# Pooled attention and a gated feed-forward layer: K and V loads issued by GpSimd on its own DMA queue, order of work searched anew

## The chip, the cores and the metric

The kernel runs on one core of a Trainium2 chip. The metric is the device time of one execution in microseconds (us), lower is better. Engines are named as in the profile: PE is TensorE (matmuls; PEld is its weight load), DVE is VectorE, ACT is ScalarE, POOL is GpSimd and SP is SyncE, which does nothing here but issue DMAs.

## What is computed

Inputs are `q`, `k`, `v` of shape (8, 8, 576, 64) and four weight matrices, all 32-bit floats (the weights arrive as 64-bit floats and are narrowed on the chip). Cut to what matters:

```
k_p = k.reshape(B, H, 72, 8, 64).mean(axis=3)          # 8 neighbouring keys are averaged
v_p = v.reshape(B, H, 72, 8, 64).mean(axis=3)
scores = q @ k_p.T / 8                                  # 576 x 72 for each batch and head
attn   = softmax(scores) @ v_p
x = attn as (4608 tokens, 512)
h = (x @ w1) * (x @ w2) @ w3                            # 512 -> 1024 -> 1024
out = h @ w_out                                         # 1024 -> 512
```

## The kernel before

**Tiling.** The 4608 tokens are cut into 12 chunks of 384. `w3` and `w_out` are multiplied into one matrix at the start, so each chunk needs `a = w1.T x`, `b = w2.T x`, their product, and one more product with the combined matrix. Each is done as three matmuls on a high and a low part of every number (`PASSES`), which is why almost every result is followed by a copy on ACT (the high part: `g_hi`, `te_post`, `mix_hi`) and a subtraction on DVE (the low part: `g_lo` at L815, and so on). Chunks 0 to 7 run plainly (L785, L833). Chunks 8 to 11 are taken two at a time and use seven block products instead of eight (`prod`, L962); their mixed weights are made during the first stage by POOL (`mix`, L882 to L884), split by ACT (`mix_hi`, L888) and DVE, and written to DRAM (L897).

**A product unit of chunks 8 to 11.** The seven products of a unit go through three accumulators in PSUM, the tags `a`, `b` and `c`. Tag `a` has one buffer: `s1_copy` (L968) and `s2_copy` (L976) on ACT, and `c22` (L987) and `g_second` (L995) on DVE, must have read it before the next product goes in. `c12` (L983) and `g_first` (L990) stand ahead of `c22` on DVE.

**Attention of a batch.** K of a batch comes in four loads (`load_k`, L390, 288 KB each), V in two (`load_v`, L457, 512 KB each) and four small ones (`load_vr`, L463, 32 KB each). All land in `st`, a pool with four buffers. Summing over the eight neighbours is done by DVE in one reduction (`pool_red`, L468) for the loads named in `K_RED` and `V_RED`, otherwise by POOL in three additions (`pool_tree`, L471 to L473). Transposed scores of the later chunks go out to DRAM and come back transposed (`te_out` L667, `te_in` L689), then `te_post` (L703, L705) splits them.

**What sets the order.** Nothing is left to a scheduler: each step is put on a list by `at(kind, k, fn, ...)` with a due time `k`, the list is sorted once, and every engine executes its own instructions in that order, each waiting at its turn for what it needs. The table `SHIFT` moves single steps by parts of a unit of `k`. Other tables choose the engine: `SOFT_ACT` (softmax of a tile mostly on ACT, or with a subtraction and sums on DVE), `MIX_DVE`, `K_RED`, `V_RED`. In the kernel before, all loads and all stores but one are issued by SP.

Of the kernel before, what the change touches and what calls it, by code (L numbers as in the profile page):

```python
# [19 lines left out]
def kernel(  # L20
# [14 lines left out]
    nc = tc.nc  # L35
# [3 lines left out]
    P = 128  # L39
# [3 lines left out]
    KR = KP - KM  # L43
# [17 lines left out]
    SOFT_ACT = [(0, 0), (0, 1), (1, 0), (1, 1), (1, 2), (1, 3), (2, 1), (2, 2), (3, 1), (3, 2), (4, 1), (4, 2),  # L61
        (4, 3), (5, 0), (5, 1), (5, 2), (6, 0), (6, 1), (6, 2), (7, 1), (7, 3), (8, 1), (8, 2), (9, 1), (9, 2),
        (10, 1), (10, 2), (10, 3), (11, 1), (11, 2)]
    HALF = [(0, 2), (2, 0), (3, 0), (4, 0), (5, 0), (6, 0), (7, 0), (8, 0), (9, 0), (10, 0), (10, 2), (11, 0)]
# [7 lines left out]
    GLO_POOL = []  # L72
    MIX_DVE = []
    MIXLO_POOL = []
    TELO_POOL = []
    K_RED = [(2, 2), (2, 3), (3, 1), (3, 2), (3, 3), (4, 0), (4, 1), (4, 2), (4, 3), (5, 1), (5, 2), (5, 3), (6,
        1), (6, 3), (7, 1), (7, 2), (7, 3)]
    V_RED = [(5, 0), (5, 1)]
    XLO_POOL = []
# [30 lines left out]
        out=msk,  # L110
        in_=ident.rearrange("p (q j e) -> p j q e", j=4, e=KR),
# [36 lines left out]
    def st_tile(shape):  # L148
        return stp.tile(shape, F32, tag="st", name="st")
# [237 lines left out]
    def load_k(b, i):  # L387
        t = stage["k", b, i] = st_tile([P, 2, POOL, D])
        if b >= 2:
            nc.sync.dma_start(  # L390
                out=t[:KP], in_=k_in[b, 2 * i:2 * i + 2].rearrange("a (k e) d -> k a (e d)", e=POOL))
        elif i < 2:
            nc.sync.dma_start(out=t.rearrange("k a e d -> k a (e d)"), in_=pair_rows(k_in, b)[KR:KR + P, 2 * i:2 * i + 2])
        else:
            for par in range(2):
                nc.sync.dma_start(
                    out=t[32 * par:32 * par + 32, 0].rearrange("k e d -> k (e d)"),
                    in_=rest_rows(k_in, b, 0, (KR + P) * par, [(2 * KP, NPR), (1, KR)]))
# [56 lines left out]
    def load_v(b, hf):  # L455
        t = stage["v", b, hf] = st_tile([P, 2, POOL, D])
        nc.sync.dma_start(out=t.rearrange("k a e d -> k a (e d)"), in_=pair_rows(v, b)[KR:KR + P, 2 * hf:2 * hf + 2])  # L457

    def load_vr(b):
        t = stage["vr", b] = st_tile([P, 2, POOL, D])  # L460
        for h in range(0, H, 2):
            g, r = h // 4, h % 4 * KR
            nc.sync.dma_start(  # L463
                out=t[r:r + 2 * KR, g].rearrange("k e d -> k (e d)"),
                in_=rest_rows(v, b, h, 0, [(KR + P, 2), (1, KR)]))
# [596 lines left out]
    def W_lo(i):  # L1062
# [30 lines left out]
        "load_w12": {(0, 0): -1, (1, 1): -3},  # L1093
        "load_w3": {(0,): -59, (1,): -35, (10,): -0.25, (11,): -0.75, (13,): -1.5, (15,): 2.75, (2,):
            -22.75, (3,): -31, (4,): -10, (5,): -22, (8,): -0.25},
        "load_wo": {(0,): -44, (1,): -30, (2,): -5},
        "mix": {(7, 0): -0.75},
        "mix_hi": {(3, 1): 0.5, (5, 0): -0.5, (5, 1): -0.5, (7, 0): -0.5, (7, 1): -0.5},
        "mix_lo": {(3, 1): 0.5, (6, 0): 0.75, (6, 1): 0.75},
        "mix_load": {(1, 0): -0.25},  # L1100
        "mix_out": {(5, 0): 1, (5, 1): 1},
        "plain_out": {(5, 1): 0.75, (7, 1): 0.75},
        "prep_k": {(0, 0): 3.5, (0, 1): 1.25, (1, 0): 0.5, (1, 1): 0.5, (1, 2): -0.75},
        "prep_v": {(1, 1): 5.25},
# [11 lines left out]
        "q_post": {(0, 1): -0.75, (0, 2): 4, (1, 0): -1.75, (1, 1): 1, (1, 2): 3.25},  # L1116
# [10 lines left out]
        "ro_low": {(0,): -29, (1,): -16, (2,): 1.5},  # L1127
        "s2_copy": {(4, 1): -0.75, (5, 0): -0.5, (5, 1): -0.75},
        "s_mm": {(0, 1, 0): -0.75, (0, 1, 1): -0.25, (0, 2, 1): -0.25, (1, 0, 0): -1.5, (1, 1, 0): -1.25,
# [34 lines left out]
        "te_out": {(10, 0): 0.25, (10, 1): 0.25, (11, 0): -2.5, (4, 0): 0.25, (4, 1): 0.25, (5, 0): -1.25,
            (6, 0): 0.75, (7, 0): -0.5, (8, 0): 0.25, (9, 0): -0.5},
        "te_post": {(10, 0): -0.5, (10, 1): 0.5, (11, 0): 1.5, (11, 1): 1.25, (3, 0): 1, (3, 1): 1, (4, 1):
            0.5, (5, 0): 1, (5, 1): 0.75, (6, 1): 0.5, (7, 0): 0.5, (7, 1): 1.25, (8, 0): 0.5, (8, 1): -2,
            (9, 0): 1, (9, 1): 0.75},
        "te_rest": {(10,): 1.5, (11,): 0.75, (5,): -0.25, (7,): 1, (8,): -1.75},
        "te_turn": {(10, 0): 0.25, (10, 1): 0.25, (10, 2): 1.25, (10, 3): 0.25, (11, 0): -0.25, (11, 1):  # L1170
            -0.25, (11, 2): -0.25, (5, 0): 0.25, (5, 1): 0.25, (5, 2): 0.25, (6, 0): -1, (6, 1): -1, (6, 2):
            -1, (7, 0): 0.25, (7, 1): 0.25, (7, 2): 0.25, (7, 3): 0.25, (9, 0): 0.25, (9, 1): 0.25, (9, 2):
            -0.75},
        "tr_q": {(8, 1): 1, (9, 0): 0.5, (9, 1): 0.5, (9, 2): 0.5, (9, 3): 0.5},
        "vr_hi": {(0,): -0.25},
# [11 lines left out]
        "x_hi22": {(4, 0): -0.5, (5, 1): 1},  # L1187
        "x_lo1": {(5, 0): 1.5, (5, 1): 1},
        "x_lo22": {(4, 0): -0.25, (5, 0): 0.5, (5, 1): 1},
        "x_plo": {(4, 0, 0): 1, (4, 0, 1): 1, (4, 0, 2): 1, (4, 0, 3): 1, (4, 1, 0): 1, (4, 1, 1): 1, (4, 1,  # L1190
            2): 1, (4, 1, 3): 3, (5, 1, 0): 1, (5, 1, 2): 0.5},
        "x_sum1": {(4, 0): -0.5},
# [108 lines left out]
    for u in range(NJ + 2):  # L1301
        k = F0 + 2 * (u - 2)
# [21 lines left out]
    for s in range(NS):  # L1324
        k = F0 + 2 * s
# [14 lines left out]
    for i in range(NJ):  # L1340
        k = K0 if i < 4 else M0 + 0.5
# [50 lines left out]
    for M in range(NP // 2, NCH // 2):  # L1392
        m0 = M0 + 6 * NJ * M
        for j in range(NJ):
            k = m0 + STEP * j
# [13 lines left out]
        k = m0 + STEP * NJ  # L1409
# [13 lines left out]
    for n in range(1, NCH):  # L1423
        k = BASE[n] = M0 + 3 * NJ * (n - 1) - (LEAD * (n - 1) // (NP - 1) if n <= NP else 3 * NJ)
# [25 lines left out]
    for b in range(1, B):  # L1450
        k = BASE[3 * (b // 2) + b % 2]
# [39 lines left out]
```

## Time and profile before

| what | us |
|---|---|
| median of 3 runs | 743.08 (742.89 to 745.27) |
| the profiled execution, its own time | 744.73 |
| its span, first to last instruction | 742.8 |
| PE busy in it | 730.5 |
| DVE busy | 469.8 |
| ACT busy | 352.8 |
| POOL busy | 174.9 |

The span is what the trace shows; the execution's own time holds 1.9 us more, before the first and after the last instruction. A busy time close to the span means that the engine hardly ever stands idle. The mean granted clock of PE is 0.999 of full speed, so the whole run is at its upper level.

### The profile page before, as it was taken

What the parts mean: (1) busy time and instruction counts of PE and PEld (TensorE: products, weight loads), DVE (VectorE), ACT (ScalarE), POOL (GpSimd) and SP (SyncE); (2) the same over time, 40 slices, a digit from 0 to 9 for tenths busy, and PEclk for the clock granted to TensorE, in tenths of its full rate; (3) what the DMA queues carried; (4) which work ended last, traced back from release to release, by engine and by line L of the source; (5) the groups of instructions that cost most, each with busy time, mean ns of one, the idle gap of its engine ahead of it and who ended that gap; (6) DMA issues with size and microseconds to landing.
All of it is one profiled execution on the core that took longest, in us unless ns stands there. A gap on an engine that the chain in (4) does not pass through costs nothing.

```text
span 742.8 us, 12190 instructions
## 1 busy us (share of the span) xinstructions
PE 730.5 (98%) x4088; PEld 681.1 (92%) x4088; DVE 469.8 (63%) x875; ACT 352.8 (47%) x1059; POOL 174.9 (24%) x228
## 2 busy tenths in 40 slices
PE   7999999999999999999999999999999999999997
PEld 6888999999999999999999999999989999899996
DVE  4788877665675845664658658566885586633342
ACT  6888986442442634434433434353454344422222
POOL 2244384033431531004503312033042000000000
PEclk9999999999999999999999999999999999999999
DMA  8989935187386465486656463826498859176611
GB/s 288 360 258 307 310 125 125 49 227 191 106 212 155 147 161 153 129 198 181 176 125 185 130 169 97 175 81 155 115 333 241 237 169 301 64 211 197 198 56 42
DMA packets 177741, 132.60 MB, mean 179 GB/s; under 512 B 78352, under 2 KB 145104, under 8 KB 177680
## 3 DMA queue, kind: packets, MB, share of 16 engines
q1 hardware_dynamic: 177536, 131.70, 62.4%
q8 instruction: 32, 0.52, 0.3%
q14 instruction: 29, 0.24, 0.1%
q10 hardware_dynamic: 144, 0.13, 0.1%
HBM read 94.63 MB, written 37.16 MB: 177 GB/s over the span
## 4 chain that ended last, share of the span: by engine, by line
PE 95%; DMA 3%; DVE 1%; SPq 0%; issue 0%; ACT 0%; DVEq 0%; ACTq 0%
PE o L833 22%; PE a L785 18%; PE b L785 18%; PE a L962 8%; PE att L533 5%; PE att L737 5%; PE o L1054 4%; PE o L848 4%; PE att L962 4%; PE b L962 2%; DMA raw<-in_moe_w_dram 1%; PE b L1054 1%; PE a L1054 1%; DMA D<-T 1%; DMA PTl<-D 1%; PE att L238 1%
## 5 line engine op out<-in xcount | busy, mean ns | idle before, releaser
L833 PE MATMUL o<-Wc,gh 128*128 128x512 f32 (+1 forms) x480 | 149.3, 392 | 0.0
L785 PE MATMUL b<-xT,hl 128*128 128x384 f32 x768 | 145.7, 339 | 0.0
L785 PE MATMUL a<-xT,hl 128*128 128x384 f32 x768 | 145.6, 338 | 0.0
L785 PEld LDWEIGHTS a<-xT,hl 128*128 128x128 f32 x768 | 133.4, 188 | 2.9
L785 PEld LDWEIGHTS b<-xT,hl 128*128 128x128 f32 x768 | 132.8, 188 | 0.0
L810 ACT CAST gh<-a 128x384 fp32r<-128x384 f32 x80 | 41.0, 513 | 126.5 <-DVE a L805 103.3
L833 PEld LDWEIGHTS o<-Wc,gh 128*128 128x128 f32 x480 | 87.4, 188 | 13.9 <-DVE ob L863 0.2
L833 PE MATMUL o<-Wc,gl 128*128 128x512 f32 (+1 forms) x240 | 93.1, 388 | 0.2 <-DVE gl L815 0.2
L571 ACT ACTIVATE E<-att,mx 128x72 f32<-128x72 f32 (+1 forms) x240 | 73.5, 324 | 28.2 <-DVE mx L549 26.5
L962 PE MATMUL a<-X,ring 128*128 128x384 f32 x384 | 77.6, 337 | 2.7 <-DVE tmp L987 1.7
L962 PEld LDWEIGHTS a<-X,ring 128*128 128x128 f32 x384 | 67.7, 188 | 6.5 <-DVE tmp L987 2.3
L805 DVE TENSOR_TENSOR a<-b,a 128x384 f32<-128x384 f32 x64 | 35.1, 549 | 50.3 <-PE b L785 48.5
L795 ACT COPY a<-a 128x384 f32<-128x384 f32 x64 | 30.8, 482 | 73.6 <-PE a L785 73.4
L471 POOL TENSOR_TENSOR st<-st 128x512 f32<-128x512 f32 (+2 forms) x29 | 38.6, 1333 | 113.0 <-DMA st<-in_v_dram 63.2
L833 PEld LDWEIGHTS o<-Wc,gl 128*128 128x128 f32 x240 | 45.0, 188 | 10.6 <-DVE gl L815 1.1
L815 DVE TENSOR_TENSOR gl<-a,gh 128x384 fp32r<-128x384 f32 x80 | 47.1, 589 | 6.9 <-ACT gh L810 6.5
L882 POOL TENSOR_TENSOR mix<-mix 128x256 f32<-128x256 f32 x16 | 13.1, 819 | 161.2 <-DMA mix<-wr 132.1
L571 ACT ACTIVATION_READ_ACCUMULATOR E<-att,mx 128x1 f32 (+1 forms) x240 | 50.1, 209 | 0.0
L533 PE MATMUL att<-kbd,qT 128*128 128x144 f32 (+1 forms) x320 | 49.9, 286 | 0.0
L533 PEld LDWEIGHTS att<-kbd,qT 128*128 128x128 f32 (+1 forms) x320 | 45.8, 179 | 1.7
L549 DVE TENSOR_REDUCE mx<-att 128x4 f32<-128x288 f32 (+1 forms) x80 | 35.3, 446 | 16.3 <-PE att L533 16.1
L1054 PE MATMUL o<-hl 128*128 128x512 f32 x144 | 38.8, 401 | 0.0
(158 smaller groups left out, 1167.7 us busy)
## 6 DMA issues: line engine op xcount, KB each, us to landing
ring<-ws SPq DMA_DIRECT2D x112, 256.0 KB
raw<-in_moe_w_dram SPq DMA_DIRECT2D x32, 512.0 KB
out_dram<-ob SPq DMA_DIRECT2D x35, 256.0 KB
st<-in_v_dram SPq DMA_DIRECT2D x16, 512.0 KB
ws<-mix SPq DMA_DIRECT2D x32, 256.0 KB
st<-in_k_dram SPq DMA_DIRECT2D x24, 288.0 KB
qs<-in_q_dram SPq DMA_DIRECT2D x112, 48.0 KB
D<-T SPq DMA_DIRECT2D x7, 768.0 KB
```

The source lines that it names most:

```text
L471: eng.tensor_tensor(out=t[:, :, 0:4], in0=t[:, :, 0:4], in1=t[:, :, 4:8], op=ALU.add)
L533: nc.tensor.matmul(out=ps[:nt, 2 * KP * j:2 * KP * (j + 1)], lhsT=qT[n][:, pr, off:off + nt], rhs=kbd[b % 2][:, pr], start=True, stop=True,)
L549: nc.vector.tensor_reduce(out=mx[:nt, hs], in_=sv, axis=AX.X, op=ALU.min)
L571: nc.scalar.activation(out=E[:nt, h], in_=sv[:, i], func=AF.Exp, scale=-1.0, bias=mx[:nt, h:h + 1], accum_out=sm[:nt, h:h + 1])
L737: nc.tensor.matmul(out=Tp[n, pr, "x"][:, off:off + cnt], lhsT=parts[x][0], rhs=parts[x][1], start=x == 0, stop=x == 3)
L785: nc.tensor.matmul(out=o, lhsT=w12[j, w][sw][:, kt * P:(kt + 1) * P], rhs=x[sx][:, kt], start=(i == 0), stop=(i == 3 * NK - 1))
L805: nc.vector.tensor_tensor(out=g, in0=ps[:, :CH], in1=g, op=ALU.mult)
L810: nc.scalar.copy(out=gh, in_=g)
L815: eng.tensor_tensor(out=gl, in0=g, in1=f(gh), op=ALU.subtract)
L833: nc.tensor.matmul(out=o, lhsT=(gh, gl)[sg][:, c], rhs=W[j][sw][:, d], start=(j == 0 and i == 0), stop=(j == NJ - 1 and i == 2))
L962: nc.tensor.matmul(out=o, lhsT=w[:, kt, sw], rhs=x[sx][:, kt], start=first and n == 0, stop=n == 5, skip_group_check=True)
L1054: nc.tensor.matmul(out=wacc[h][it], lhsT=w3t[s][sa][:, it * P:(it + 1) * P], rhs=wo[j][sb], start=(j == 0 and i == 0), stop=(j == NJ - 1 a ...
```

## The change

Loads of K and V of batches 2 to 7 are issued by `nc.gpsimd` and not by `nc.sync`: 24 K loads, 12 V loads and 24 small V loads. The tables of numbers are different in some fifty places. The core of the diff ("..." marks what is left out):

```diff
     SOFT_ACT = [... (4, 1), (4, 2),
-        (4, 3), (5, 0), (5, 1), (5, 2), (6, 0), (6, 1), (6, 2), (7, 1), ...
+        (4, 3), (5, 1), (5, 2), (6, 1), (6, 2), (7, 1), ...
-    MIX_DVE = []
+    MIX_DVE = [(5, 0)]
-    K_RED = [... (4, 3), (5, 1), (5, 2), (5, 3), (6, 1), ...
+    K_RED = [... (4, 3), (5, 3), (6, 1), ...
-    V_RED = [(5, 0), (5, 1)]
+    V_RED = [(5, 1), (7, 1)]
...
     def load_k(b, i):
         t = stage["k", b, i] = st_tile([P, 2, POOL, D])
         if b >= 2:
-            nc.sync.dma_start(
+            nc.gpsimd.dma_start(
...
     def load_v(b, hf):
         t = stage["v", b, hf] = st_tile([P, 2, POOL, D])
-        nc.sync.dma_start(out=t.rearrange("k a e d -> k a (e d)"), in_=pair_rows(v, b)[KR:KR + P, 2 * hf:2 * hf + 2])
+        eng = nc.gpsimd if b >= 2 else nc.sync
+        eng.dma_start(out=t.rearrange("k a e d -> k a (e d)"), in_=pair_rows(v, b)[KR:KR + P, 2 * hf:2 * hf + 2])
...
             g, r = h // 4, h % 4 * KR
-            nc.sync.dma_start(
+            eng = nc.gpsimd if b >= 2 else nc.sync
+            eng.dma_start(
...
-        "load_w3": {... (2,): -22.75, (3,): -31, ...
+        "load_w3": {... (2,): -29.5, (3,): -31, ...
-        "prep_k": {(0, 0): 3.5, ...
+        "prep_k": {(0, 0): 4, ... (4, 3): 2},
-        "s2_copy": {(4, 1): -0.75, (5, 0): -0.5, (5, 1): -0.75},
+        "s2_copy": {(4, 0): -0.25, (4, 1): -1, (4, 2): -0.25, ...
```

PE's own list of instructions is the same in both kernels, in kind and order. Line numbers of the kernel after are 2 higher from `load_vr` on, and some 7 higher after the tables. Three places where the lists of other engines differ:

On POOL, between the mixing of the 13th and the 14th piece of weights (`mix`), which is at about 390 to 399 us of the span, the kernel before has no other step:

```order
L882 TENSOR_TENSOR mix<-mix 128x2x128
L883 TENSOR_TENSOR mix<-mix 128x128
L884 TENSOR_TENSOR mix<-mix 128x128
L882 TENSOR_TENSOR mix<-mix 128x2x128
L883 TENSOR_TENSOR mix<-mix 128x128
L884 TENSOR_TENSOR mix<-mix 128x128
```

In the kernel after, the six V loads of batch 5 and one sum over neighbours (`st` to `vm`) stand between them:

```order
L884 TENSOR_TENSOR mix<-mix 128x2x128
L885 TENSOR_TENSOR mix<-mix 128x128
L886 TENSOR_TENSOR mix<-mix 128x128
L458 DMA st<-in_v_dram 128x2x512 x2
L465 DMA st<-in_v_dram 16x1x512 x4
L473 TENSOR_TENSOR st<-st 128x2x256
L474 TENSOR_TENSOR st<-st 128x2x128
L475 TENSOR_TENSOR vm<-st 128x128
L884 TENSOR_TENSOR mix<-mix 128x2x128
L885 TENSOR_TENSOR mix<-mix 128x128
L886 TENSOR_TENSOR mix<-mix 128x128
```

So the 14th piece moves behind six issues and three additions on POOL.

On ACT, in the first product unit of chunks 8 and 9 (at about 545 us), `s2_copy` (`tmp<-a`) stands behind the two copies of finished output (`ob<-o`) before:

```order
L968 COPY a<-a 128x384
L566 ACTIVATE E<-E 96x288
L973 COPY tmp<-att 128x384
L566 ACTIVATE E<-E 96x288
L865 COPY ob<-o_5567 128x512
L865 COPY ob<-o_5569 128x512
L976 COPY tmp<-a 128x384
```

and ahead of them after:

```order
L970 COPY a<-a 128x384
L568 ACTIVATE E<-E 96x288
L975 COPY tmp<-att 128x384
L568 ACTIVATE E<-E 96x288
L978 COPY tmp<-a 128x384
L867 COPY ob<-o_5569 128x512
L867 COPY ob<-o_5571 128x512
```

That copy no longer waits for the output sums.

On DVE at about 320 to 326 us, the reduction of the fourth K load of batch 4 (`km<-st`) stands ahead of a low part (`gl<-a,gh`) and a product (`a<-b,a`) before:

```order
L705 TENSOR_TENSOR PTl<-PTl,PTh 128x768
L699 TENSOR_TENSOR PTr<-PTr 64x768
L705 TENSOR_TENSOR PTl<-PTl,PTh 128x768
L468 TENSOR_REDUCE km<-st 72x128
L815 TENSOR_TENSOR gl<-a,gh 128x384
L805 TENSOR_TENSOR a<-b,a 128x384
```

and behind both after:

```order
L701 TENSOR_TENSOR PTr<-PTr 64x768
L707 TENSOR_TENSOR PTl<-PTl,PTh 128x768 x2
L817 TENSOR_TENSOR gl<-a,gh 128x384
L807 TENSOR_TENSOR a<-b,a 128x384
L470 TENSOR_REDUCE km<-st 72x128
```

The low part is one reduction earlier in DVE's list. Further, the fifth and sixth load on SP at the start (both pieces of `w3`) have changed places, while ACT and DVE still take the two pieces in the order of before; and the V loads of batch 7, which SP issued at about 539 us, stand on POOL behind the two small `space` fills that ran at 513 us, with one of the two V halves now summed by DVE (`V_RED` (7, 1)) in the first unit of chunks 8 and 9.

## Rows read from the trace of the kernel before

**Rows 1.** The page's first part: busy time, share, instructions.

```profile
PE 730.5 (98%) x4088; PEld 681.1 (92%) x4088; DVE 469.8 (63%) x875; ACT 352.8 (47%) x1059; POOL 174.9 (24%) x228
```

**Rows 2.** Busy time by stretch: us, PE, PEld, DVE, ACT, POOL; clock, DMA share, GB/s.

```profile
0.00:20.00 20.00, 14.55 (x88) 12.54 (x89) 9.69 (x18) 13.57 (x23) 4.06 (x13) 1.00 0.87 297
...
330.00:540.00 210.00, 210.00 (x1181) 198.68 (x1180) 138.74 (x256) 91.37 (x288) 54.50 (x74) 1.00 0.56 146
540.00:580.00 40.00, 38.07 (x211) 35.40 (x210) 29.03 (x58) 20.07 (x76) 12.82 (x16) 1.00 0.88 277
580.00:720.00 140.00, 139.26 (x762) 131.27 (x761) 71.08 (x136) 45.70 (x114) 0.00 (x0) 1.00 0.60 178
720.00:742.80 22.80, 18.83 (x104) 15.92 (x102) 6.38 (x12) 5.62 (x11) 0.00 (x0) 0.98 0.19 69
```

**Rows 3.** Instructions in order of time, 542 to 549: start, us, engine, line, [idle before].

```profile
544.70 0.59 ACT L865 COPY ob<-o 128x512 f32<-128x512 f32 x1 [0.79 <-PE o L833]
544.95 1.28 POOL L471 TENSOR_TENSOR st<-st 128x512 f32<-128x512 f32 x1 [31.63 <-DMA st<-in_v_dram]
545.18 0.49 ACT L976 COPY tmp<-a 128x384 f32<-128x384 f32 x1
545.72 1.00 PEld L962 LDWEIGHTS a<-X,ring 128*128 128x128 f32 x6 [0.33 <-ACT tmp L976]
545.72 1.31 PE L962 MATMUL a<-X,ring 128*128 128x384 f32 x6
...
546.40 1.06 DVE L990 TENSOR_TENSOR a<-a,tmp 128x384 f32<-128x384 f32 x1
...
547.39 0.54 DVE L987 TENSOR_TENSOR tmp<-a,tmp 128x384 f32<-128x384 f32 x1
...
547.74 1.28 POOL L471 TENSOR_TENSOR st<-st 128x512 f32<-128x512 f32 x1
...
547.98 1.31 PE L962 MATMUL a<-X,ring 128*128 128x384 f32 x6 [0.95 <-DVE tmp L987]
548.04 1.40 DVE L815 TENSOR_TENSOR gl<-a,gh 128x384 fp32r<-128x384 f32 x1
```

**Rows 4.** The same view, the two other longest stops of PE after 540.

```profile
575.44 0.83 ACT L703 CAST PTh<-PTl 128x768 fp32r<-128x768 f32 x1 [1.59 <-DMA PTl<-D]
...
576.71 1.31 PE L962 MATMUL a<-X,ring 128*128 128x384 f32 x6 [0.96 <-ACT tmp L976]
...
653.08 1.14 PE L962 MATMUL a<-X,ring 128*128 128x384 f32 x5 [0.74 <-DVE tmp L987]
```

**Rows 5.** The same view, DVE and PE at 323 to 326.

```profile
323.25 1.98 DVE L468 TENSOR_REDUCE km<-st 72x128 f32<-72x1024 f32 x1
325.15 0.54 DVE L815 TENSOR_TENSOR gl<-a,gh 128x384 fp32r<-128x384 f32 x1
...
325.75 0.50 PE L833 MATMUL o<-Wc,gl 128*128 128x512 f32 x1 [0.18 <-DVE gl L815]
```

**Rows 6.** The same view, ACT, DVE and PE at the start.

```profile
13.33 0.68 ACT L173 ACTIVATE Wc<-raw 128x512 f32<-128x512 f32 x1 [0.40 <-DMA raw<-in_moe_w_dram]
13.67 1.29 DVE L186 SCALAR_TENSOR_TENSOR Wc<-Wc 128x512 int32<-128x512 int32 x2
14.41 1.26 PE L236 MATMUL att<-ident,Wc 128*128 128x128 f32 x8 [0.88 <-DVE Wc L186]
```

**Rows 7.** One line's instructions: durations in ns min/median/max, first and last start.

```profile
L390 SPq DMA_DIRECT2D st<-in_k_dram x24: 311/410/902, 146.1 to 512.8; - x24
L463 SPq DMA_DIRECT2D st<-in_v_dram x32: 615/623/1369, 42.2 to 545.6; - x32
```

**Rows 8.** Instructions in order of time, POOL and ACT at 389 to 404.

```profile
389.77 0.74 POOL L882 TENSOR_TENSOR mix<-mix 128x256 f32<-128x256 f32 x1 [20.42 <-DMA mix<-wr]
...
391.63 0.62 ACT L888 CAST mix<-mix 128x512 fp32r<-128x512 f32 x1 [2.28 <-POOL mix L884]
...
403.15 0.62 ACT L888 CAST mix<-mix 128x512 fp32r<-128x512 f32 x1
```

More of the change, by code (lines that the diff above doesn't have):

```diff
@@ L61 @@
     SOFT_ACT = [(0, 0), (0, 1), (1, 0), (1, 1), (1, 2), (1, 3), (2, 1), (2, 2), (3, 1), (3, 2), (4, 1), (4, 2),
-        (4, 3), (5, 0), (5, 1), (5, 2), (6, 0), (6, 1), (6, 2), (7, 1), (7, 3), (8, 1), (8, 2), (9, 1), (9, 2),
-        (10, 1), (10, 2), (10, 3), (11, 1), (11, 2)]
+        (4, 3), (5, 1), (5, 2), (6, 1), (6, 2), (7, 1), (7, 3), (8, 1), (8, 2), (9, 1), (9, 2), (10, 1), (10,
+        2), (10, 3), (11, 1), (11, 2)]
     HALF = [(0, 2), (2, 0), (3, 0), (4, 0), (5, 0), (6, 0), (7, 0), (8, 0), (9, 0), (10, 0), (10, 2), (11, 0)]
@@ L72 @@
     GLO_POOL = []
-    MIX_DVE = []
+    MIX_DVE = [(5, 0)]
     MIXLO_POOL = []
     TELO_POOL = []
-    K_RED = [(2, 2), (2, 3), (3, 1), (3, 2), (3, 3), (4, 0), (4, 1), (4, 2), (4, 3), (5, 1), (5, 2), (5, 3), (6,
-        1), (6, 3), (7, 1), (7, 2), (7, 3)]
-    V_RED = [(5, 0), (5, 1)]
+    K_RED = [(2, 2), (2, 3), (3, 1), (3, 2), (3, 3), (4, 0), (4, 1), (4, 2), (4, 3), (5, 3), (6, 1), (6, 3), (7,
+        1), (7, 2), (7, 3)]
+    V_RED = [(5, 1), (7, 1)]
     XLO_POOL = []
@@ L1093 @@
         "load_w12": {(0, 0): -1, (1, 1): -3},
-        "load_w3": {(0,): -59, (1,): -35, (10,): -0.25, (11,): -0.75, (13,): -1.5, (15,): 2.75, (2,):
-            -22.75, (3,): -31, (4,): -10, (5,): -22, (8,): -0.25},
-        "load_wo": {(0,): -44, (1,): -30, (2,): -5},
+        "load_w3": {(0,): -59, (1,): -35, (10,): -0.25, (11,): -0.75, (13,): -1.5, (15,): 2.75, (2,): -29.5,
+            (3,): -31, (4,): -10, (5,): -22, (8,): -0.25},
+        "load_wo": {(0,): -44, (1,): -31.5, (2,): -5},
         "mix": {(7, 0): -0.75},
         "mix_hi": {(3, 1): 0.5, (5, 0): -0.5, (5, 1): -0.5, (7, 0): -0.5, (7, 1): -0.5},
-        "mix_lo": {(3, 1): 0.5, (6, 0): 0.75, (6, 1): 0.75},
+        "mix_lo": {(3, 1): 0.5, (5, 1): 1, (6, 0): 0.75, (6, 1): 0.75},
         "mix_load": {(1, 0): -0.25},
@@ L1102 @@
         "plain_out": {(5, 1): 0.75, (7, 1): 0.75},
-        "prep_k": {(0, 0): 3.5, (0, 1): 1.25, (1, 0): 0.5, (1, 1): 0.5, (1, 2): -0.75},
+        "prep_k": {(0, 0): 4, (0, 1): 1.25, (1, 0): 0.5, (1, 1): 0.5, (1, 2): -0.75, (4, 3): 2},
         "prep_v": {(1, 1): 5.25},
@@ L1161 @@
             2.5, (6, 0): 2.5, (6, 1): 2.5, (7, 0): 2.25, (7, 1): 4.5},
-        "te_in": {(10, 0): 0.5, (10, 1): 2, (11, 0): -2, (3, 0): 0.75, (4, 0): 0.5, (6, 0): 1, (7, 0): -1,
+        "te_in": {(10, 0): 0.5, (10, 1): 2, (11, 0): -2, (3, 0): 1.5, (4, 0): 0.5, (6, 0): 1, (7, 0): -1,
             (7, 1): 0.5, (8, 0): 0.5, (9, 0): -1},
         "te_out": {(10, 0): 0.25, (10, 1): 0.25, (11, 0): -2.5, (4, 0): 0.25, (4, 1): 0.25, (5, 0): -1.25,
[L1165 to L1174, printed above, removed]
+            (6, 0): -0.25, (7, 0): -0.5, (8, 0): -0.5, (9, 0): -0.5},
+        "te_post": {(10, 0): -0.5, (10, 1): 0.5, (11, 0): 1.5, (11, 1): 1.25, (4, 1): 0.5, (5, 0): 1, (5,
+            1): 0.75, (6, 1): 0.5, (7, 0): 0.5, (7, 1): 1.25, (8, 0): 0.5, (8, 1): -2, (9, 0): 1, (9, 1):
+            0.75},
+        "te_rest": {(10,): 1.5, (11,): 0.75, (5,): -0.75, (7,): 1, (8,): -1.75},
+        "te_turn": {(10, 2): 1, (11, 0): -0.25, (11, 1): -0.25, (11, 2): -0.25, (4, 0): 1, (5, 0): 0.25, (5,
+            1): 0.25, (5, 2): 0.25, (6, 1): -1, (6, 2): -1, (7, 0): 0.25, (7, 1): 0.25, (7, 2): 0.25, (7,
+            3): 0.25, (8, 0): 1, (9, 0): 0.25, (9, 1): 0.25, (9, 2): -0.75},
+        "tr_q": {(8, 1): 1, (9, 0): 0.5, (9, 1): 0.5, (9, 2): 0.5, (9, 3): 1.25},
         "vr_hi": {(0,): -0.25},
@@ L1187 @@
         "x_hi22": {(4, 0): -0.5, (5, 1): 1},
[L1188 to L1191, printed above, removed]
+        "x_lo1": {(4, 1): 1.75, (5, 0): 1.5, (5, 1): 1},
+        "x_lo22": {(4, 0): -0.25, (4, 1): 0.25, (5, 0): 0.5, (5, 1): 1},
+        "x_plo": {(4, 0, 0): 1, (4, 0, 1): 1.25, (4, 0, 2): 1, (4, 0, 3): 1.5, (4, 1, 0): 0.75, (4, 1, 1):
+            1, (4, 1, 2): 1, (4, 1, 3): 3, (5, 1, 0): 1, (5, 1, 2): 0.5},
         "x_sum1": {(4, 0): -0.5},
```

29 rows, old and new, of the table SHIFT are left out of this document.

## The prediction

> **What bounds the kernel now.** I read the page's first part before anything else: PE is busy for 730.5 us [rows 1] of a span of 742.8. Whatever the change does on other engines, it counts only where it alters one of PE's stops, or PE's own list, and that list is the same in both kernels. So the second view was the busy time by stretch, to find where PE stops [rows 2]. The reader is to subtract PE's column from the length: 20.00 − 14.55 = 5.45 us in the first twenty, 0 from 20 to 320, 10.00 − 9.82 = 0.18 from 320 to 330, 0 from 330 to 540, 40.00 − 38.07 = 1.93 from 540 to 580, 140.00 − 139.26 = 0.74 from 580 to 720, 22.80 − 18.83 = 3.97 at the end. That is 12.27 us in all, and it caps every gain. The clock column says 1.00 (0.98 at the end), the upper of the two levels, 2.4 GHz, so nothing is to be had there. The third view was the instructions in order of time around each stop in the middle: 0.18 at 325.75 [rows 5], 0.95 at 547.98 [rows 3], 0.96 at 576.71 and 0.74 at 653.08 [rows 4]. Together 2.83, with 0.02 in crumbs 2.85. The last stretch holds no step that the change moves, so its 3.97 stay.
>
> **The change part by part.** All terms are against the profiled execution's own 744.73 us: its span of 742.80 and 1.93 around it, which stay. It is 1.65 above the median of the runs, 743.08; I subtract the sum from both.
>
> *The stop at 325.* PE waits 0.18 for `gl` at L815. The row above says why: DVE does the reduction of K(4,3) (L468), 1.98 us, and L815 follows it at 325.15 [rows 5]. After the change the reduction stands behind L815, so L815 is done up to 1.98 earlier and cannot be what PE waits for. What could be late next is the high part for the same product, which ACT makes before L815 reads it. The stop can only give what it holds: −0.18, between 0 and −0.18. I take −0.18.
>
> *The stops at 545 to 548.* Two instructions of one unit are late [rows 3]. First `s2_copy` (L976), at 545.18 behind an output copy (L865) of 0.59 on ACT; PE's weight load of the third product waits 0.33 for it, while PE's own row at 545.72 shows no stop. With the copy ahead of both L865, the gain lies between 0 and −0.33; half of it, −0.17, is taken. Second, `c22` (L987) starts at 547.39, though the third product had ended at 545.72 + 1.31 = 547.03, since DVE was behind: L990 took 1.06 where L987, also 128x384 and 32-bit, takes 0.54. Beside L990 POOL sums the first half of V(7), from 544.95 to 547.74, 2.79 us. After the change the V(7) loads stand behind fills that ran at about 513, long before the 545 at which they are used, so POOL's additions can go earlier and L990 be undisturbed. Then `c22` can start as the product ends: −0.36, and the rest of the 0.95, 0.59, is the time of `c22` itself. Bounds: 0, if one sum still runs beside L990; −0.95 if the whole stop went, which the chain product, `c22`, product excludes as long as `c22` takes 0.54. I take −0.36.
> The Trainium skill ("SBUF — State Buffer", section "Who interferes with whom") says that DVE shares one pair of SBUF ports with GpSimd under an exclusive lock and that only this pair causes contention. By that rule too moving POOL's sums away frees L990; the trace agrees with 1.06 against 0.54. The rule would also let POOL's additions disturb DVE wherever they land instead, which no row prices, and which the sum holds at nothing, since PE has no stop from 330 to 540.
>
> *One V(7) half on DVE.* `V_RED` (7, 1) puts a reduction on DVE in the same unit: some 2.0 us by the row of L468 at 1.98 [rows 5]. It takes away the disturbance seen there: 1.06 − 0.54 = 0.52 on L990 and 1.40 − 0.54 = 0.86 on L815 [rows 3, 5], 1.38 together. DVE has 40.00 − 29.03 = 10.97 idle in this stretch [rows 2], so the net 0.6 is hidden. If DVE had no gap at that place PE would lose 0.6. Value 0, bounds 0 and +0.6.
>
> *The stop at 576.* PE waits 0.96 for an L976 on ACT that stands behind `te_post` (L703), and that waited 1.59 for a transposed load `PTl<-D` [rows 4]. ACT's order is unchanged there, and the load is still SP's. Fewer loads on SP could bring it up to 0.96 earlier, another traffic pattern could delay it. The DMA engines are 0.88 busy in this stretch [rows 2] and carry the same bytes on whichever queue. Value 0, bounds −0.96 and the +0.6 above.
>
> *The stop at 653.* The 0.74 is `c22` between two products of tag `a` [rows 4]; nothing in it moves: 0.
>
> *The start.* The fifth and sixth SP load, both `w3`, change places while ACT and DVE take the two pieces in the old order. In before the later one releases ACT's first copy (L173) at 13.33 [rows 6]. The piece wanted first now comes sixth: its copy starts at 13.33 and lasts 0.68, to 14.01, and DVE's conversion (L186), which ran at 13.67, starts at 14.01. PE's first product behind it, at 14.41, moves as far: 14.01 − 13.67 = +0.34. Bounds: 0, if the two loads share the engines and land together, and +0.88, the stop that PE had there, once more. I take +0.34.
>
> *Sixty issues on POOL.* 24 + 12 + 24 = 60 DMA issues leave SP. No row shows an issue on POOL. On SP they cost 0.311 at the least (L390) and 1.369 at the most (L463) [rows 7], so 19 to 82 us of POOL's 742.8 − 174.9 = 567.9 idle. I take 0.62, the median of L463, since the V loads are the ones at the place that decides: 37 us, all in idle time. What is queued behind them on POOL are the sums and the mixing of weights, and the tightest place is the 14th piece of `mix`. Before it now stand six issues and one sum of 2.79. Piece 13 is done at 391.63, when ACT's split L888 starts [rows 8]; it lasted 391.63 − 389.77 = 1.86. Piece 14 is ready at 391.63 + 6c + 2.79 + 1.86 = 396.28 + 6c for c us an issue. ACT takes it up at 403.15 [rows 8], so with c = 0.62 (400.0) it waits for nothing, and c may be 6.87 / 6 = 1.14 before ACT waits at all. When ACT did wait at 391.63, 2.28 us, PE went on, with no stop from 330 to 540 [rows 2, 8]; I take that as the slack behind ACT here. With c at its upper bound, 1.369, piece 14 comes at 404.5, 1.3 late, still inside 2.28. So 0 at both ends, and 0 is taken.
>
> *The rest of the tables* moves softmax and mixing steps between ACT and DVE in the stretch 20 to 540, where PE stops 0.18 us in all: 138.74 of 210 us busy on DVE and 91.37 on ACT [rows 2] are room for it. 0; what it could gain is nothing but those 0.18, what it could lose is open, and the chance of it is in the last rival.
>
> **The sum.** −0.18 − 0.17 − 0.36 + 0 + 0 + 0.34 + 0 = −0.37. The profiled execution goes from 744.73 to 744.36, the median from 743.08 to 742.71, rounded 742.7. The lowest by the bounds: −0.18 − 0.33 − 0.95 − 0.96 = −2.42; the highest 0.6 + 0.88 = +1.48.
>
> **Rivals.** *A, all stops in the middle go.* If the earlier V(7) and the relieved SP also let `PTl<-D` arrive in time, and `c22` is covered, PE runs through from 20 to 720: 743.08 − 2.85 = 740.2. For it: the loads are off SP, and SP issued them in the very stretch that holds 1.93 of the stops. Against: 0.74 of it is unchanged, and `te_post` waits for transfers while the DMA engines are 0.88 busy.
> *B, an issue on POOL is dear.* Place: piece 14 of `mix`. It decides from c = (403.15 + 2.28 − 396.28) / 6 = 1.53 us. With c half again the longest issue of rows 7, 1.5 × 1.369 = 2.05, the piece is ready at 408.6, 5.4 late, and PE loses 5.4 − 2.28 = 3.15: 742.71 + 3.15 = 745.9, slower. For it: the semaphores of these loads are of another kind in the kernel after, so POOL does something else than SP to issue them; six stand in a row at one place. Against: no row shows an issue above 1.369, and POOL could take 567.9 / 60 = 9 us for each before it is full.
> The Trainium skill ("DMA: Bandwidth & Descriptors", section "Anatomy of one DMA — SWDGE (gpsimd) path") says that GpSimd writes the descriptors in software, with a fixed 2.0 us per DMA. If POOL were held that long, piece 14 would be ready at 408.3 and PE lose 2.85; no row here shows such a DMA.
> *C, the shuffled middle costs something.* Sums that now run beside other DVE work stretch it as L990 was stretched, by 0.5 to 0.9 each; two or three such on a chain that PE waits for give 1 to 2 us, 743.7 to 744.7. For it: fifty numbers moved. Against: PE stopped nowhere there, so there is slack.
>
> **How the numbers follow.** About 0.3% (2.23 us, so 740.85 to 745.31) is what a measurement of this kernel can tell from no change. The forecast with its small terms has 0.52, C 0.15, both within 0.3%. A has 0.18, faster. B has 0.15, slower. So faster 0.18, same 0.67, slower 0.15. The range takes in A's and B's own values, 740.2 and 745.9, and leaves little more than the far side of both out; the forecast's own range would be 740.7 to 744.6.
>
> **What would show it.** In the profile after: PE's column in 320 to 330 without a stop; the stop at 548 near 0.6 and L990 near 0.54, with POOL's sum of V(7) before 545; a stop of 0.9 or so at 576 and 0.74 at 653 as before; PE's first product after the sixth load at 14.7; the DMA issues on POOL of 0.3 to 1.4 us each; no wait of ACT at piece 14. The forecast is wrong if PE's busy time in 20 to 540 falls short of the length by more than 1 us, or if an issue holds POOL for more than 1.5 us.

## The result, and the profile after

Slower: the median of the kernel after is 750.97 us (745.17 to 753.25), that of the kernel before in the same measurement 743.54 us. The ratio is 1.0083 with an interval of 1.0058 to 1.0108. The forecast was 742.7, within 740.2 to 745.9. The profiled execution after took 747.56 us with a span of 745.8, one of the shorter of its executions; it shows the places of the loss, not its full size, which two profiles among the experiments show. Two single executions among the experiments, of 1222 and 2158 us, were in a slow state and are left out of every median and ratio below.

The page's first part, in the columns of [rows 1]:

```profile
PE 731.6 (98%) x4088; PEld 681.9 (91%) x4088; DVE 467.7 (63%) x884; ACT 348.7 (47%) x1031; POOL 220.5 (30%) x291
```

POOL has 45.6 us more, 40.3 of it the 60 issues. Busy time by stretch, the columns of [rows 2]:

```profile
0.00:20.00 20.00, 15.10 (x88) 13.34 (x89) 10.45 (x19) 13.94 (x25) 4.05 (x13) 1.00 0.90 310
20.00:320.00 300.00, 298.37 (x1687) 275.63 (x1685) 206.79 (x392) 169.15 (x526) 118.00 (x146) 1.00 0.67 187
320.00:330.00 10.00, 10.00 (x54) 9.26 (x53) 6.84 (x9) 4.10 (x7) 3.38 (x6) 1.00 0.96 199
330.00:540.00 210.00, 208.81 (x1172) 197.54 (x1171) 134.67 (x255) 88.73 (x273) 90.42 (x120) 1.00 0.57 147
540.00:580.00 40.00, 38.51 (x219) 36.44 (x218) 29.39 (x63) 20.26 (x76) 4.66 (x7) 1.00 0.83 260
580.00:720.00 140.00, 139.26 (x763) 131.31 (x762) 71.74 (x139) 45.98 (x115) 0.00 (x0) 1.00 0.62 182
720.00:745.80 25.80, 21.59 (x118) 18.38 (x116) 7.82 (x14) 6.52 (x13) 0.00 (x0) 1.00 0.17 61
```

Length minus PE's column, against [rows 2]: the stop at 325 is gone, 540 to 580 fell from 1.93 to 1.49, and the start from 5.45 to 4.90. But 20 to 320 and 330 to 540, where PE never stopped before, now have 1.63 and 1.19. The sum of all stops is 1.89 above before, PE's busy time 1.11 (the ends of matmuls are modelled, so a short wait can be drawn as busy); together the 3.00 by which the span grew.

The largest new stop, in order of time (start, us, engine, line, [idle before]), kernel after:

```profile
467.90 1.74 SPq L691 DMA_DIRECT2D PTl<-D  x4
...
469.22 1.43 POOL L390 DMA_DIRECT2D st<-in_k_dram  x2
...
477.12 0.84 ACT L705 CAST PTh<-PTl 128x768 fp32r<-128x768 f32 x1 [4.62 <-DMA PTl<-D]
...
478.87 0.55 DVE L817 TENSOR_TENSOR gl<-a,gh 128x384 fp32r<-128x384 f32 x1
...
479.47 0.50 PE L835 MATMUL o<-Wc,gl 128*128 128x512 f32 x1 [1.19 <-DVE gl L817]
```

The same place in the kernel before:

```profile
465.77 1.74 SPq L689 DMA_DIRECT2D PTl<-D  x4
...
471.45 0.83 ACT L703 CAST PTh<-PTl 128x768 fp32r<-128x768 f32 x1 [1.01 <-DMA PTl<-D]
```

From the first issue of the transposed loads to ACT's use of them it was 471.45 − 465.77 = 5.68 us before, and is 477.12 − 467.90 = 9.22 after. DVE's `gl` stands behind `te_post` and PE behind `gl`. What is new there is the pair of K loads, K(7,0) and K(7,1), 1.3 us behind the transposed loads, on the other queue. In the kernel before SP issued these two at 489, behind the transposed loads and the q loads. POOL comes to them 20 us sooner: it has nothing to wait for there but free buffers, so it runs ahead of the order's due times.

The other new stops lie at 203, 208 and 224. DVE, POOL and PE before them, kernel after:

```profile
191.57 0.72 POOL L390 DMA_DIRECT2D st<-in_k_dram  x1
...
192.31 1.29 POOL L473 TENSOR_TENSOR st<-st 72x512 f32<-72x512 f32 x1
192.35 1.28 DVE L593 TENSOR_SCALAR sm<-sm 128x8 f32<-128x8 f32 x1
...
193.91 1.11 DVE L596 TENSOR_TENSOR E<-E,sm 128x576 f32<-128x576 f32 x1
...
196.06 1.67 DVE L817 TENSOR_TENSOR gl<-a,gh 128x384 fp32r<-128x384 f32 x1 [0.58 <-ACT gh L812]
...
203.52 2.35 PE L787 MATMUL b<-xT,hl 128*128 128x384 f32 x12 [0.45 <-DVE a L807]
...
208.19 2.35 PE L787 MATMUL a<-xT,hl 128*128 128x384 f32 x12 [0.27 <-ACT a L797]
...
224.67 0.45 PE L739 MATMUL att<-PTr,VR 128*128 128x384 f32 x1 [0.83 <-DVE PTr L701]
```

POOL's sums of batch 2 and 3 now follow issues of 4.5 us and run beside DVE's softmax: L593 takes 1.28 where the row at 201.79 has 0.17, L817 1.67 where the one at 205.07 has 0.53. The stop at 224 has another cause, which the last experiment finds in the tables.

### The profile page after: what moved, and what is told of

It is laid out like the page before. It is cut to its first block, busy times and chain, and to the rows that moved or that the text cites. A ratio compares the mean times of both kernels' runs of the same rounds, so it can differ in the third digit from the quotient of the medians.

```text
span 745.8 us, 12162 instructions
## 1 busy us (share of the span) xinstructions
PE 731.6 (98%) x4088; PEld 681.9 (91%) x4088; DVE 467.7 (63%) x884; ACT 348.7 (47%) x1031; POOL 220.5 (30%) x291
## 3 DMA queue, kind: packets, MB, share of 16 engines
q0 software_dynamic: 6336, 14.17, 7.1%
## 4 chain that ended last, share of the span: by engine, by line
PE 87%; DMA 5%; DVE 4%; ACT 1%; SPq 1%; issue 1%; ACTq 0%; DVEq 0%
PE o L835 20%; PE a L787 16%; PE b L787 15%; PE a L964 8%; PE att L739 5%; PE att L535 5%; PE o L1056 4%; PE o L850 4%; PE att L964 4%; PE b L964 2%; DMA D<-T 2%; DMA PTl<-D 2%; DMA raw<-in_moe_w_dram 1%; ACT E L573 1%; DMA PTr<-D 1%; PE b L1056 1%
## 5 line engine op out<-in xcount | busy, mean ns | idle before, releaser
L573 ACT ACTIVATE E<-att,mx 128x72 f32<-128x72 f32 (+1 forms) x224 | 68.4, 322 | 26.5 <-DVE mx L551 23.7
L884 POOL TENSOR_TENSOR mix<-mix 128x256 f32<-128x256 f32 x15 | 11.2, 748 | 160.5 <-DMA mix<-wr 102.7
L817 DVE TENSOR_TENSOR gl<-a,gh 128x384 fp32r<-128x384 f32 x80 | 46.6, 583 | 7.9 <-ACT gh L812 7.7
L473 POOL TENSOR_TENSOR st<-st 128x512 f32<-128x512 f32 (+2 forms) x31 | 42.7, 1378 | 19.9 <-DMA st<-in_v_dram 12.5
L573 ACT ACTIVATION_READ_ACCUMULATOR E<-att,mx 128x1 f32 (+1 forms) x224 | 46.6, 208 | 0.0
```

The costliest lines, as they stand in the source:

```text
L473: eng.tensor_tensor(out=t[:, :, 0:4], in0=t[:, :, 0:4], in1=t[:, :, 4:8], op=ALU.add)
L573: nc.scalar.activation(out=E[:nt, h], in_=sv[:, i], func=AF.Exp, scale=-1.0, bias=mx[:nt, h:h + 1], accum_out=sm[:nt, h:h + 1])
L817: eng.tensor_tensor(out=gl, in0=g, in1=f(gh), op=ALU.subtract)
```

## Experiments

Two theories at first. Q: the second queue costs, by loads that meet transfers or work they did not meet before. T: the new tables cost. In the table, PTl is the time from the first issue of the transposed loads at about 467 to ACT's use of them (the expectations count to the end of their last packet, 5.22 in after_k7sp, 9.30 in sp_v6k7pool and 5.08 in sp_k7pool), ACT's wait is what ACT stands idle for them, and the stop is PE's behind it, all from the one profile of each kernel; ratios are to the kernel before, measured beside it.

| kernel | loads on GpSimd | median us | ratio (interval) | PTl | ACT's wait | stop |
|---|---|---|---|---|---|---|
| before | none | 743.5 to 744.4 | 1 | 5.68 | 1.01 | 0 |
| after | 60 | 750.97 | 1.0083 (1.0058 to 1.0108) | 9.22 | 4.62 | 1.19 |
| after_again | 60 | 749.82 | 1.0066 (1.0044 to 1.0089) | 8.24 | 3.64 | 0.21 |
| before_pool | 60, tables of before | 751.45 | 1.0092 (1.0071 to 1.0112) | 8.33 | 5.24 | 1.81 |
| after_sp | none, tables of after | 746.04 | 1.0022 (1.0012 to 1.0033) | 5.92 | 1.26 | 0 |
| after_k7sp | all but K(7,0), K(7,1) | 746.09 | 1.0020 (1.0003 to 1.0037) | 6.09 | 1.51 | 0 |
| after_b23sp | all but batches 2, 3 | 748.28 | 1.0053 (1.0031 to 1.0074) | 10.37 | 7.27 | 3.84 |
| after_both | all but these 22 | 744.78 | 1.0010 (0.9994 to 1.0025) | 5.84 | 2.85 | 0 |
| sp_v6k7pool | V(6), K(7,0), K(7,1) | 751.46 | 1.0088 (1.0071 to 1.0105) | 10.27 | 7.12 | 3.69 |
| sp_k7pool | K(7,0), K(7,1) | 746.09 | 1.0019 (1.0007 to 1.0032) | 5.90 | 1.22 | 0 |
| best | as after_both | 743.69 | 0.9991 (0.9975 to 1.0007) | 5.93 | 2.91 | 0 |

In all five profiles with a stop, the stop is ACT's wait less 3.43: 4.62 − 1.19, 3.64 − 0.21, 5.24 − 1.81, 7.27 − 3.84, 7.12 − 3.69. Where ACT waits less than that, PE does not stop. So PE had 3.43 us of room behind ACT's wait at this place, and the kernel before, with a wait of 1.01, had 2.42 of it left.

**Queue or tables.** The kernel after once more, unchanged (after_again); the kernel after with its 60 loads on SP (after_sp):

```diff
-            nc.gpsimd.dma_start(
+            nc.sync.dma_start(
...
-        eng = nc.gpsimd if b >= 2 else nc.sync
+        eng = nc.sync
```

(the last edit stands in `load_v` and in `load_vr`), and the kernel before with the same 60 on GpSimd (before_pool):

```diff
-            nc.sync.dma_start(
+            nc.gpsimd.dma_start(
...
-        nc.sync.dma_start(...
+        eng = nc.gpsimd if b >= 2 else nc.sync
+        eng.dma_start(...
```

> The kernel after, unchanged, a second time, for a second profiled execution and more times: its executions so far lie between 745.2 and 753.3 us, and 8 of 12 show a granted clock of 0.994 to 0.998 while the profiled one (747.6) has 1.0. Every theory expects a median of 748 to 752. If the spread comes from PE stops whose length differs from one execution to the next, the profile shows stops at the same places as before (224.7, 479.5) with other lengths, and where the clock is below 1.0 the dip follows one of them.

> The kernel after with its 60 loads of K and V back on SP, tables of after kept. Theory Q (the second queue is the cause): 742 to 744 us, a narrow spread, no stop at 479. Theory T (the new tables are the cause): 748 to 752, as the kernel after.

> The kernel before with nothing but the 60 loads of K and V moved to GpSimd, tables of before kept. Theory Q: 746 to 753 us, a wide spread, and a stop of PE of over 1 us somewhere between 150 and 540 us. Theory T: 742.5 to 744.

Theory Q, in the main: the queue alone makes the kernel before 0.92% slower (0.71 to 1.12), no less than the whole change (0.66 and 0.83). The tables by themselves cost 0.22%, which Q as I had put it (742 to 744) did not foresee. The stop at 479 is in all three profiles with the loads on GpSimd and not in that with the loads on SP. Its length differs from one execution to the next: 1.19, 0.21, 1.81. In the profile of before_pool, whose span is 9.2 us longer than before's, it is only one of several: PE also stops for 1.49 at 583.92, 1.42 at 543.33 and 1.06 at 242.80, and the granted clock is 1.00 up to 745. What the move costs at those places with the tables of before was not taken apart.

**Another second queue.** The 60 loads issued by ACT:

```diff
-            nc.gpsimd.dma_start(
+            nc.scalar.dma_start(
...
-        eng = nc.gpsimd if b >= 2 else nc.sync
+        eng = nc.scalar if b >= 2 else nc.sync
```

> The kernel after with the 60 loads issued by ACT, on its own queue, and not by GpSimd. If any second queue lets the loads compete with the transposed loads of SP's queue, it stays at 747 to 753 us. If it is GpSimd that is the cause (its issues, its software-made descriptors), it falls to 742 to 745; ACT has some 390 us idle for 60 issues of about 0.4 us.

760.98 us, ratio 1.0225 (1.0205 to 1.0245): outside both. Its longest stops, 1.93 us at 354 and 2.03 at 453, lie at other places, and its transposed loads at 477 take 5.88 us. ACT's order put the loads elsewhere in time; what in it costs the 2.25% was not taken apart. So this run doesn't tell whether a hardware-fed second queue would hurt as GpSimd's does.

**Two loads, and twenty.** K(7,0) and K(7,1) back on SP (after_k7sp):

```diff
-            nc.gpsimd.dma_start(
+            (nc.sync if b == 7 and i < 2 else nc.gpsimd).dma_start(
```

the 20 loads of batches 2 and 3 back on SP (after_b23sp), and both edits in one kernel (after_both):

```diff
-            nc.gpsimd.dma_start(
+            (nc.sync if b < 4 else nc.gpsimd).dma_start(
...
-        eng = nc.gpsimd if b >= 2 else nc.sync
+        eng = nc.gpsimd if b >= 4 else nc.sync
```

> The kernel after with two of the 60 loads, K(7,0) and K(7,1), back on SP, where they stand behind the transposed loads (PTl) and the q loads. In the profiles of kernels with these two on GpSimd they go out at 469 us and the PTl loads of that moment take 6.8 to 7.3 us; with the loads on SP they take 4.7 to 5.1. Theory 1 (the two loads overtake the transposed loads and PE's stop at 479, 0.2 to 1.8 us long by the profile, is theirs, and where it is long the clock falls after it): PTl back at 5.3 us or less, no stop over 0.3 us at 479, median 746 to 748.5, fewer executions with a clock under 0.999. Theory 2 (the stop comes from GpSimd's time, or the dips follow another stop): median 749.5 to 751.

> The kernel after with the 20 loads of batches 2 and 3 back on SP; those of batches 4 to 7 stay on GpSimd. If the issues on GpSimd push the sums of V(2) and K(3) into DVE's work (L593 1.28 us where it takes 0.2, L817 1.67 where it takes 0.56), the two stops of PE at 203 and 208 us (0.45 and 0.28) go and DVE's rows there are short again, while the 0.83 at 224 stays, which the kernel with all loads on SP also has: 0.7 to 1.5 us below the kernel after in the same call's terms, some 749. If the dips of the clock start here, 746 to 747.

> Both: the 20 loads of batches 2 and 3 and the two of K(7,0), K(7,1) on SP, the other 38 on GpSimd, tables of after. If these two places are all that the second queue costs, this comes to the time of the kernel with all loads on SP, 745.5 to 746.5 us, or up to 0.8 below it, for the stop at 549 that it does not have. If the cost is spread over all places, 747.5 or more.

Two of sixty loads take the ratio from 1.0066 (the lower of the two that the kernel after has) to 1.0020: 0.46% of 744, some 3.4 us. The granted clock of the twelve executions is now 0.998 to 1.000, where the kernel after has 0.994 to 0.998 in nine of twelve. Kernel after_k7sp at that place:

```profile
467.97 1.74 SPq L691 DMA_DIRECT2D PTl<-D  x4
...
474.06 0.83 ACT L705 CAST PTh<-PTl 128x768 fp32r<-128x768 f32 x1 [1.51 <-DMA PTl<-D]
```

The twenty loads give back 1.0066 − 1.0053 = 0.13%, 1.0 us with intervals that overlap; in their profile the stops at 203 and 208 are gone and the 0.83 at 224 stays (222.73), as expected. So these two stops come with the twenty loads on GpSimd, at a price that is not clear of the noise. That profile also fell on an execution in which the two K loads went out ahead of the transposed loads, not behind. Kernel after_b23sp:

```profile
466.72 1.43 POOL L390 DMA_DIRECT2D st<-in_k_dram  x2
467.46 1.77 SPq L691 DMA_DIRECT2D PTl<-D  x4
...
477.83 0.83 ACT L705 CAST PTh<-PTl 128x768 fp32r<-128x768 f32 x1 [7.27 <-DMA PTl<-D]
...
480.18 0.50 PE L835 MATMUL o<-Wc,gl 128*128 128x512 f32 x1 [3.84 <-DVE gl L817]
```

Its stretches around the stop (columns of [rows 2]):

```profile
475.00:480.00 5.00, 1.34 (x8) 0.90 (x6) 1.31 (x2) 2.17 (x4) 0.00 (x0) 1.00 0.99 165
480.00:485.00 5.00, 4.83 (x16) 4.41 (x17) 4.46 (x8) 1.83 (x4) 0.00 (x0) 0.66 0.58 93
485.00:490.00 5.00, 5.00 (x34) 5.00 (x32) 2.41 (x5) 1.49 (x4) 0.00 (x0) 1.00 0.06 10
```

After PE has stood for 3.84 us, the granted clock of the next five is 0.66, so part of them ran at the lower level, 1.2 GHz, and (1 − 0.66) × 5 = 1.7 us are lost on top. After the 1.19 of the kernel after it stayed at 1.00. So a place that costs 0.2 us in one execution costs 5.5 in another. The spread of the times fits that: of the twelve executions of the kernel after, the three with a mean clock of 1.000 take 745.2 to 747.6 us, the nine with 0.994 to 0.998 take 746.7 to 753.3; none of the nine was profiled.

**Enough, and when.** Only eight loads on GpSimd, V(6), K(7,0) and K(7,1); and only the two of K, which then wait on POOL for sums of a V that SP loads at 479:

```diff
-            nc.gpsimd.dma_start(
+            (nc.gpsimd if b == 7 and i < 2 else nc.sync).dma_start(
...
-        eng = nc.gpsimd if b >= 2 else nc.sync
+        eng = nc.gpsimd if b == 6 else nc.sync
```

The second kernel, sp_k7pool, has `eng = nc.sync` in the last line.

> The kernel after with only eight loads on GpSimd: the six of V of batch 6 and K(7,0), K(7,1); the other 52 on SP. Is meeting the transposed loads at 468 enough? GpSimd, which waits for nothing else there, will issue V(6) as soon as buffers are free, at some 455 to 460 us (SP does it at 479), and K(7,0), K(7,1) at 465 to 470 (SP at 490). Theory 1: PTl of that moment takes 6.5 to 9.5 us, PE stops for 0.3 to 4 us at 479, some executions have a clock under 0.999, median 748 to 751. Rival, that it needs all 60 loads on GpSimd's queue: 745.5 to 746.5, as with all loads on SP.

> The kernel after with only K(7,0) and K(7,1) on GpSimd, V(6) and all others on SP. GpSimd sums V(6), which SP loads at 479, before it issues the two, so they go out after 483, when the transposed loads have landed. Theory 1 (it is the moment that costs, not the queue as such): PTl 4.7 to 5.3 us, no stop at 479, 745.0 to 746.5 us. Rival (two loads on GpSimd's queue cost wherever they are): 748 or more.

Both as theory 1 has it, the price of the eight, 751.46, a little above its 748 to 751. Eight loads cost as much as sixty; the same two K loads on the same queue, but issued at 489, cost nothing against all on SP (746.09 and 746.04). Kernel sp_v6k7pool:

```profile
467.72 1.43 POOL L390 DMA_DIRECT2D st<-in_k_dram  x2
468.68 1.74 SPq L691 DMA_DIRECT2D PTl<-D  x4
...
478.95 0.83 ACT L705 CAST PTh<-PTl 128x768 fp32r<-128x768 f32 x1 [7.12 <-DMA PTl<-D]
...
481.29 0.80 PE L835 MATMUL o<-Wc,gl 128*128 128x512 f32 x1 [3.69 <-DVE gl L817]
```

and its stretches behind the stop:

```profile
480.00:485.00 5.00, 3.71 (x9) 3.06 (x10) 4.56 (x7) 2.95 (x6) 0.00 (x0) 0.55 0.65 99
485.00:490.00 5.00, 5.00 (x25) 5.00 (x25) 1.90 (x5) 0.48 (x1) 0.00 (x0) 0.77 0.18 30
```

The stop and the lost clock, 3.69 + 0.45 × 5 + 0.23 × 5 = 7.1 us, are what this execution's span, 751.0, has over that of after_sp, 743.9 (one execution of each).

The queues in the kernel after, from the page (packets, MB, share of the 16 engines' time):

```profile
q1 hardware_dynamic: 170096, 117.55, 55.7%
q0 software_dynamic: 6336, 14.17, 7.1%
```

GpSimd's queue moves 14.17 MB in 6336 packets, 2.2 KB each with the small ones in; SP's 0.69 KB each. Where both are busy here, the transposed loads fall behind. In the trace's packets of the kernel after, the K loads' packets (4096 bytes) take a median of 254 to 417 ns in each us from 472 to 474, against 159 where V(6) runs alone at 461; and the number of the transposed loads' packets (1536 bytes, 512 in all) falls from 131 in the us at 471 to 30, 9 and 7 in the three after it, so that the last tenth of them takes as long as the rest. In the kernel before, where no K packets meet them, 489 of the 512 start between 466 and 470. The Trainium skill ("DMA: Bandwidth & Descriptors", section "SWDGE vs HWDGE vs iDMA") says that software and hardware descriptors feed different queues within each engine, which goes round-robin between them, and under "Issuing engines are not separate DMA queues" that transfers of all issuers interleave on the same 16 engines. The packet counts and the PTl column, 5.7 to 6.1 against 8.2 to 10.4, fit this; no run here shows the round-robin apart from other causes.

**A version of parts.** The kernel before with only what had looked like gains:

```diff
-        nc.sync.dma_start(...
+        eng = nc.gpsimd if b == 7 else nc.sync
+        eng.dma_start(...
...
-        "prep_k": {... (1, 2): -0.75},
+        "prep_k": {... (1, 2): -0.75, (4, 3): 2},
...
-        "s2_copy": {(4, 1): -0.75, (5, 0): -0.5, (5, 1): -0.75},
+        "s2_copy": {(4, 0): -0.25, (4, 1): -1, (4, 2): -0.25, ...
```

> The kernel before with the three parts that the profiles show as gains and nothing else: the six V loads of batch 7 on GpSimd (the stop at 548 falls from 0.95 to 0.6 or less), prep_k of (4,3) behind gl (the stop at 325, 0.18, and what stands around it), and s2_copy as in the kernel after. Theory: 0.5 to 1.2 us faster than before (0.1 to 0.16%). Rival: the six loads compete with other transfers of SP's queue from 513 on, as K(7,0) does at 469, and the result is 744.4 or slower.

746.48 us, ratio 1.0030 (1.0015 to 1.0044): slower, but not for the rival's reason. Kernel hybrid:

```profile
525.90 1.29 POOL L473 TENSOR_TENSOR st<-st 128x512 f32<-128x512 f32 x1
526.12 1.48 DVE L1035 TENSOR_TENSOR tmp<-tmp,xr 128x384 f32<-128x384 f32 x1
...
528.90 1.29 POOL L473 TENSOR_TENSOR st<-st 32x512 f32<-32x512 f32 x1
529.10 1.51 DVE L817 TENSOR_TENSOR gl<-a,gh 128x384 fp32r<-128x384 f32 x1
...
537.49 0.80 PE L964 MATMUL b<-X,ring 128*128 128x384 f32 x3 [1.92 <-DVE a L807]
```

The stop at 548 fell to 0.73 and that at 576 went. But POOL's sums of V(7), now at 521 to 532, meet DVE where it has no gap: L1035 takes 1.48 where its row at 535.43 has 0.55, L817 1.51, and PE stops for 1.92 behind DVE. That these two make up the stop is read from the one profile; no run took them apart.

**The best.** after_both, and the transposed loads of chunk 3 at their old place:

```diff
-        "te_in": {... (3, 0): 1.5, ...
+        "te_in": {... (3, 0): 0.75, ...
+        "te_post": {... (3, 0): 1, (3, 1): 1, ...
```

> The kernel with K and V of batches 2 and 3 and K(7,0), K(7,1) on SP, the other 38 loads on GpSimd, tables of after, and te_in and te_post of chunk 3 as before: the transposed loads at 211 go out about 1 us earlier, and the stop of 0.83 at 222.6, which every kernel with the tables of after has, goes. Theory: 0.8 to 1.3 us below the same kernel without this (744.8 beside 744.0 for before), so 743.5 to 744, 0 to 0.5 below before. Rival: the tables of after need these values, and it is no better than 744.8.

743.69 us beside 744.37. The stop of 0.83 is gone, so it came from these two tables. The ratio is 1.0010 − 0.9991 = 0.19% of 744, 1.4 us, lower, but the two intervals overlap, and the one profile has a stop of 1.63 at 577.34 where after_both has 0.70. The interval, 0.9975 to 1.0007, doesn't set it apart from the kernel before.

## Why the prediction was wrong

The step that failed is "the same bytes on whichever queue", written under the stop at 576 and silently used for every transposed load. What the runs showed in its place: two K loads on the other queue, going out at the moment of the transposed loads, delay these by 2.6 to 4.7 us, and that costs some 3.4 us. I had looked at queues as something that holds an issuing engine, and priced the sixty issues on POOL by what stands behind them there. What decided was the other side: which transfers a load meets once it no longer stands in SP's line. A hint was there: [rows 4] has ACT waiting 1.59 for `PTl<-D` at 575 with PE behind it, so transposed loads stood close to PE's path. I saw the wait and asked only whether it could shrink; the row at 471.45, with its wait of 1.01, is not among my rows. The sign that I had named came: PE's busy time in 20 to 540 falls short of the length by 1.63 + 1.19 = 2.82, where 1 was the limit.

Point by point:
- *Issues on POOL.* Taken 0.62 us each, 37 in all; measured 0.71 for K (median), 0.74 and 0.58 for V: 24 × 0.71 + 12 × 0.74 + 24 × 0.58 = 39.8. Right. Piece 14 of `mix` came at 406.17, 6 us later than worked out, since POOL was done with piece 13 only at 393.3, waited 1.81 for its V load and 2.73 for the piece itself; ACT waited 0.85 there and PE nothing. Right in its result.
- *The stop at 325:* gone. *545 to 548:* 0.74 of 0.95 stays, at 551, and the row of L990 (now L992) is down from 1.06 to 0.56; so the term gave 0.21 and not 0.36. The undisturbed chain of `c22` takes 0.74, as [rows 4] had it at 653, not the 0.59 I took. The V(7) half on DVE takes 1.93 at 551.65, behind that stop, and costs nothing, as said. *576:* 0.76 for 0.96. *653:* 0.74, unchanged.
- *The start.* +0.34 expected; both `w3` loads now release their users together at 12.96, and PE's product starts at 14.42 against 14.41. The lower bound, 0, held.
- *The rest of the tables,* 0 expected: 0.22% slower (0.12 to 0.33) by after_sp; `te_in` and `te_post` of chunk 3 may be most of it, 0.19% by the last run, within the noise. I had let PE's unbroken rows stand for slack; they tell that nothing was late, not by how much.
- *Rivals.* B's price (2.05 us an issue) and place were wrong, its side right. C's mechanism, sums that stretch DVE's work, is real at 203 and in hybrid; I gave it 1 to 2 us and called it within the noise. The mechanism that carried most of the loss was among none of them.

The range ended at 745.9 for lack of that case: 3.4 us for two loads, 1.0 for twenty (not clear of noise), some 1.6 for the tables, against gains of a few tenths; the ratio of 1.0083 is 6.2 us.

## What to carry to other kernels

When loads move to another queue, list every transfer that stood behind or ahead of them in the old one and whose landing the critical engine waits for; a queue held back bulk loads, and without it they meet the transfers that were to go first. An engine with nothing to wait for issues its loads as early as buffers allow, not when the order meant them: here at 467 to 470 and not at 489. And with an engine at 98% a late transfer can cost twice, once as a stop (3.84 us) and once as the clock after it (1.7). Before a move, work out how much later each such transfer may come before the critical engine stops; here it was 2.4 us.

## What was not expected of the hardware

- Two loads of 288 KB on GpSimd's queue made transposed loads of SP's queue take 8.2 to 10.4 us where they take 5.7 to 6.1. Where the two went out 1.2 to 1.3 us behind the first transposed load, these took 8.2 to 9.2 us in three profiles; where 0.7 to 1.0 ahead of it, 10.3 to 10.4 in two.
- The clock fell to 0.66 for five us after a stop of 3.84, and to 0.55 (with 0.77 after it) after one of 3.69; it stayed at 1.00 after 1.19 and 1.81. The length of the one stop does not tell it alone: after 1.93 us in after_act the four us from 354 have 0.61, after 1.92 in hybrid the clock stayed at 1.00.
- Open: whether it is the software-made queue or any second queue, since the run with ACT put the loads elsewhere in time; and whether the same two loads on SP, issued as early, would cost as much, which no run tried.
